# Pair 0's operand sums and remainders in halves on VectorE and GpSimd, layer one's on VectorE

## The chip, the cores and the metric

The kernel runs on one core of a Trainium2 chip. The metric is the device time of one execution in microseconds (us); lower is better. The engines are TensorE (PE in the profile, its weight loads PEld), VectorE (DVE), ScalarE (ACT), GpSimd (POOL) and SyncE (SP), whose queue starts nearly all DMAs.

## The reference

Sparse attention, then two dense layers, all in float32:

```python
scores = scale * q @ k.T                     # 4 batches, 8 heads, 576 positions, 64 wide
thresh = max(scores) - tau                   # per row
scores = where(scores >= thresh, scores, -1e9)
attn = softmax(scores); x = attn @ v         # x becomes 2304 tokens x 512
x = ((x @ w_a) * (x @ w_b)) @ w_out          # layer one, 1536 hidden
h = x @ w_in                                 # layer two, 1024 hidden
solu = h * softmax(h)
out = (layer_norm(solu) * g_ln) @ w_out2
```

## The kernel before

Attention handles two heads of one batch at a time in nine tiles of scores, and works them off two tiles to a step: 144 tiles, steps m = 0 to 77, scores up to step 71. In a step the engines work as follows. PE makes two tiles of scores (L586), the products with v of an older step (PV, L668) and the transposes of the step before (L637). DVE reduces each score tile out of PSUM into SBUF and finds its row minimum of the negated scores (`soft_max`, L591). ACT takes the exponential (L603). GpSimd makes a threshold of one column from the minimum (`soft_thr`, L608). DVE then masks (`soft_mask`, L617): scores and exponentials, both in SBUF, are compared with the threshold, multiplied and summed. The order of emission within a step is the string `PROG = 'ABtuVFTUYXfab'`: A and B are scores, reduction and exponential of the two tiles, t and u the thresholds, f the place for side work, a and b the masks.

Every float32 product of layer one is made from numbers split into a rounded high part and a remainder, so that three matmuls stand for one. Layer one uses Strassen's scheme with seven products (`product`, L510). The tokens are handled in three pairs of blocks of 384 columns. A pair's operands are made by normalising x (`norm_ops`, L386, L391, L395), four sums (`sum_ops`, L420), seven high parts on ACT and seven remainders (`operand_ops`, L444 and L448), and the seven are also stored for reuse (`store_op`). A sum or remainder covers 2 x 384 = 768 columns. The weights are converted from raw words, differenced (L276) and split (`split_ops`, L233 and L236).

Pair 0's operands are made during attention. Loads of x and of the softmax sums are issued at step 46. The pieces stand in the string `SLOTS` (n normalisation, s sum, h high part, l remainder, o store, z and x the loads of pair 1), and from step 52 on each step takes from its front: up to one piece of DVE, two of GpSimd, and one of ACT. A piece marked "DP" (VectorE or GpSimd) goes to GpSimd here. Pair 1's normalisation is appended at step 72 and runs two to a step. The conversion of the weights of layer one's first blocks is emitted at the end of steps 6 to 77 (`conv_emit`), its DVE part in `fill`.

In layer one (`moe1`) the order of the products, of the copies out of PSUM and of the gating multiplications is written out by unit n = 0 to 35; everything else is a task with a due time, which a planner (`bg`, `step`, `force`) places on the engines it may use, by a model of their costs and clocks. Pairs 1 and 2 get their operands there, and so do the weights after the first. A "DP" piece goes to whichever of the two engines the planner finds free. Each engine runs its instructions in the order of emission.

Of the kernel before, what the change touches and what calls it, by code (L numbers as in the profile page):

```python
# [17 lines left out]
P = 128  # L18
# [3 lines left out]
def kernel(  # L22
# [186 lines left out]
    def stage_ops(got, dst, low_of):  # L209
# [18 lines left out]
            return [("A", 512, expo), ("D", 300, low), ("D", 512, sign), ("D", 512, join)]  # L228
        return [("A", 512, lambda: nc.scalar.activation(out=dst(), in_=got["raw"], func=AF.Copy))]

    def split_ops(dst, src, n):
        def hi():
            nc.scalar.activation(out=dst(0), in_=src(), func=AF.Copy)  # L233

        def lo(e):
            (nc.vector if e == "D" else nc.gpsimd).tensor_tensor(out=dst(1), in0=src(), in1=dst(0).bitcast(F32), op=ALU.subtract)  # L236

        return ("A", n, hi), ("DP", n, lo)

    own = {}  # L240
    last = {}
# [8 lines left out]
    def ab_tasks(f, due, at, stage_at=0, bufs=("a", "t"), deps=()):  # L250
        ba, bt = bufs
        got = {}
        deps = list(deps) + [last[b] for b in bufs if b in last]
        la, lb = (load_w(w1[f, :, i], due - 16 + i, stage_at) for i in range(2))

        def view(b):
            if b not in got:
                got[b] = buffer(b).rearrange("p (o h c) -> p o h c", o=2, h=2)
            return got[b]

        def flat(b, i):
            return view(b)[:, i].rearrange("p h c -> p (h c)")

        def wt(o, u):
            if f not in wst:
                wst[f] = pools["w" if f % 4 < FW else "w4"].tile([P, 7, 2, QK * P], F32R, tag="w", name=f"w1_{f}")
            return wst[f][:, o, u, :]

        ta = task(due - 12, stage_ops(la["got"], lambda: flat(ba, 0), lambda: flat(bt, 0)), [la["load"]] + deps)
        tb = task(due - 10, stage_ops(lb["got"], lambda: flat(ba, 1), lambda: flat(bt, 0)), [lb["load"], ta])  # L270
        la["used"], lb["used"] = ta, tb
        a = lambda: view(ba)
        t = lambda: view(bt).rearrange("p o h c -> p (o h) c")

        def diff(n, out, x, y):
            return ("DP", n, lambda e: (nc.vector if e == "D" else nc.gpsimd).tensor_tensor(out=out(), in0=x(), in1=y(), op=ALU.subtract))  # L276

        td = task(due - 7, [
            diff(512, lambda: t()[:, 0:2], lambda: a()[:, 1], lambda: a()[:, :, 0, :]),
            diff(256, lambda: t()[:, 2], lambda: a()[:, 1, 1], lambda: t()[:, 0]),  # L280
            diff(256, lambda: t()[:, 3], lambda: a()[:, 0, 1], lambda: t()[:, 2]),
        ], [tb])
        parts = [
            split_ops(lambda u: wt(slice(0, 2), u), lambda: a()[:, 0], 512),
            split_ops(lambda u: wt(slice(3, 5), u), lambda: t()[:, 0:2], 512),
            split_ops(lambda u: wt(2, u), lambda: a()[:, 1, 1], 256),
            split_ops(lambda u: wt(slice(5, 7), u), lambda: t()[:, 2:4], 512),
        ]
        ready_w[f] = [task(due, [hi, lo], [td], at) for hi, lo in parts]
        end = task(due, [("S", 0, lambda: None)], ready_w[f], at)  # L290
        for b in bufs:
            last[b] = end
        return end
# [111 lines left out]
    def quad(p, i, k):  # L405
        return xs[p][:, k * QK:(k + 1) * QK, i * H:(i + 1) * H]

    def sum_ops(s, p):
        def one(k, e):
            if k == 0:  # L410
                scs[s] = own["sc"].rearrange("p (s k c) -> p s k c", s=4, k=QK)
            a11, a12, a21, a22 = (quad(p, i, h) for i in range(2) for h in range(2))
            z = scs[s]
            out, a, b, op = (
                (0, a21, a22, ALU.add),
                (1, z[:, 0], a11, ALU.subtract),
                (3, a12, z[:, 1], ALU.subtract),
                (2, a11, a21, ALU.subtract),
            )[k]
            (nc.vector if e == "D" else nc.gpsimd).tensor_tensor(out=z[:, out], in0=a, in1=b, op=op)  # L420

        return [("DP", QK * H, lambda e, k=k: one(k, e)) for k in range(4)]

    ORDER = [(s, j) for s in range(SETS[-1] + 1) for j in range(7) if s <= NPR or s % 2 or j > 1]
    GATE = (-1, -1, 0, 1, 2, 4, 6)
# [9 lines left out]
            own["x2"] = raw_p.tile([P, 2, QK, 2, H], F32R, tag="xr0", name="xt2")  # L435
        return own["x2"][:, j]

    def operand_ops(s, j, p):
        def src():
            return scs[s][:, (0, 0, 0, 1, 3, 2)[j]] if j in (1, 3, 4, 5) else quad(p, j // 6, min(j // 2, 1))  # L440

        def hi():
            xts[s, j] = new_xt(s, j)
            nc.scalar.activation(out=xts[s, j][:, :, 0, :], in_=src(), func=AF.Copy)  # L444

        def lo(e):
            x = xts[s, j]
            (nc.vector if e == "D" else nc.gpsimd).tensor_tensor(out=x[:, :, 1, :], in0=src(), in1=x[:, :, 0, :].bitcast(F32), op=ALU.subtract)  # L448

        return [("A", QK * H, hi), ("DP", QK * H, lo)]  # L450

    def store_op(s, j, p):
        nc.sync.dma_start(out=opd[p][j], in_=xts[s, j].bitcast(F32))
# [74 lines left out]

    def attention():
        es, es_r = ExitStack(), ExitStack()  # L530
        slots = []
        conv_ops = conv_first()
        ps_a = es.enter_context(tc.tile_pool(name="ps_a", bufs=3, space=PSUM))
        px = es.enter_context(tc.tile_pool(name="px", bufs=2))
# [76 lines left out]
        def soft_mask(i, s, th):  # L611
            ns, pe = st[i, s]
            if s == 0:
                st[i, "z"] = sm.tile([P, NS], F32, name="z", bufs=2)
            z = st[i, "z"]
            pv = pe.rearrange("p (g s) -> p g s", g=2)
            nc.vector.scalar_tensor_tensor(out=pv, in0=ns, scalar=th, in1=pv, op0=ALU.is_le, op1=ALU.mult, accum_out=z[:, s:s + 1])  # L617
            st[i, s] = pe

        def recip(i):  # L620
# [117 lines left out]
                    conv_emit("D")  # L738

        conv_at = range(6, tot // 2 + 6)  # L740
        PROG = 'ABtuVFTUYXfab'
        SLOTS = "n0 n1 n2 n3 s0 h0 l0 h1 o0 l1 h2 o1 l2 s1 o2 s2 h3 l3 h4 o3 s3 l4 h5 o4 l5 h6 z0 o5 l6 x0 o6"
        for m in range(tot // 2 + 6):
            if m == 46:
                load_z(0)
                load_x(0)
                ops = {"n": norm_ops(0), "s": sum_ops(0, 0), "z": [("S", 0, lambda: load_z(1))], "x": [("S", 0, lambda: load_x(1))]}
                ops["h"], ops["l"] = zip(*(operand_ops(0, j, 0) for j in range(NX)))
                ops["o"] = [("S", 0, lambda j=j: store_op(0, j, 0)) for j in range(NX)]
                slots = [ops[w[0]][int(w[1])] for w in SLOTS.split()]  # L750
                late = norm_ops(1)
            if m == tot // 2:
                es_s.close()
# [33 lines left out]
            for ch in PROG:  # L787
                if ch in "AB":
                    score("AB".index(ch))
                elif ch == "V":  # L790
                    for mm in mms:
                        mm()
                elif ch == "F":
                    for j in range(NP):
                        if m - j * NS // 2 == 8:
                            finish(j)
                elif ch in "TU":
                    turn("TU".index(ch))
                elif ch == "Y":
                    for c in old:  # L800
                        tpose_tail(*c)
                elif ch in "tu":
                    thr("tu".index(ch))
                elif ch in "ab":
                    mask("ab".index(ch))
                elif ch == "X":
                    if m == tot // 2:
                        for j in range(3):
                            product(0, 0, j)
                elif ch == "f":  # L810
                    fill(len(lo_old))
                    quota = {"D": 1, "P": 2, "A": 1, "S": 9}
                    if m == tot // 2:
                        slots += late
                        alloc_x(2)
                        quota["D"] = 2
                    while m >= 52 and slots and quota[slots[0][0][-1]]:
                        engs, _, fn = slots.pop(0)
                        eng = engs[-1]
                        quota[eng] -= 1  # L820
                        if len(engs) > 1:
                            fn = lambda fn=fn: fn("P")
                        if eng in "AS":
                            evac_q.append(fn)
                        else:
                            fn()
                        if eng == "A":
                            break
                    fill(1)
            for fn in dma_q + later:  # L830
                fn()
            dma_q.clear()
# [14 lines left out]
                    step(t)  # L847
            if m in conv_at:
                conv_emit("AP", 3)
        conv_emit("ADP", len(conv_ops))  # L850
        for t in ready_w[FW]:
            force(t)
        for engs, _, fn in slots:
            fn("P") if len(engs) > 1 else fn()
        for t in tasks:
            t["end"] = 0.0
        for e in clock:
# [24 lines left out]
    def moe1():  # L882
# [2 lines left out]
        gp = es.enter_context(tc.tile_pool(name="gp", bufs=1))  # L885
        yp = es.enter_context(tc.tile_pool(name="yp", bufs=4))
        groups = []
        ysteps = []
        stores = []

# [346 lines left out]
```

## Time and profile before

| | |
|---|---|
| median of 3 runs | 945.89 us (945.88 to 945.93) |
| the profiled execution | 946.57 us, of which the span in the profile is 944.8 us |
| PE busy | 908.5 us, 96% of the span |
| DVE busy | 654.3 us, 69% |
| ACT busy | 471.9 us, 50% |
| POOL busy | 283.0 us, 30% |

Times in the profile count from the start of the span. A busy PE is not a PE at its peak, since matmuls are pipelined and their ends are modelled. In the timelines a line gives start, duration, engine, line of the kernel, operation, output<-inputs, shape, count, and in brackets how long the engine had been idle and what ended that. Durations of neighbours on DVE overlap a little.

### The profile page before, as it was taken

Reading aid. Unit: us, or ns where it says so; the run is one execution under the profiler, and the core shown is the slowest. Engines: PE = TensorE matmul, PEld = TensorE weight load, DVE = VectorE, ACT = ScalarE, POOL = GpSimd, SP = SyncE. Lnnn points to the kernel's source line nnn. Section 1 sums busy time; section 2 is a strip of 40 time slices with the busy share of each in tenths; the row PEclk is TensorE's granted clock in tenths of the full one; section 3 lists DMA queues with packets and bytes.
Section 4 is the critical chain, followed back from the end, with each engine's and each line's share of the span. In section 5 each row is a group of like instructions: output and inputs, shape, how many; then the busy total and the mean of one; then the engine's idle time right before and its main releaser. Section 6 shows DMA issues by size and latency. Waiting matters only on the chain.

```text
span 944.8 us, 16336 instructions
## 1 busy us (share of the span) xinstructions
PE 908.5 (96%) x5896; PEld 752.5 (80%) x5896; DVE 654.3 (69%) x1359; ACT 471.9 (50%) x886; POOL 283.0 (30%) x347
## 2 busy tenths in 40 slices
PE   7999999998898788999999999999999899999998
PEld 3555565654468788999999999999998788888886
DVE  6999988899876775675668666876676544444443
ACT  5887877876775363543233323433342433333332
POOL 1255321136426352321023102110033433333330
PEclk9999999999999898999999999999999899999999
DMA  6435333845714847459765788568875011111100
GB/s 174 147 102 164 120 109 95 200 120 200 237 63 145 248 158 280 151 172 353 288 231 169 263 299 291 185 203 323 290 245 165 23 45 46 45 44 45 45 23 34
DMA packets 78481, 154.54 MB, mean 164 GB/s; under 512 B 11840, under 2 KB 51392, under 8 KB 78400
## 3 DMA queue, kind: packets, MB, share of 16 engines
q1 hardware_dynamic: 77600, 152.81, 48.9%
q8 instruction: 47, 0.77, 0.3%
q10 hardware_dynamic: 800, 0.68, 0.3%
q14 instruction: 34, 0.28, 0.1%
HBM read 108.55 MB, written 44.92 MB: 162 GB/s over the span
## 4 chain that ended last, share of the span: by engine, by line
PE 87%; DVE 7%; DMA 2%; issue 1%; ACT 1%; ACTq 0%; SPq 0%; POOL 0%; DVEq 0%; POOLq 0%
PE acc L510 26%; PE py L933 15%; PE po L1144 10%; PE ps L1088 9%; PE po L668 8%; PE ps L586 8%; PE tp L637 7%; DVE pe L617 3%; PE pl L1125 2%; PE py L510 1%; DVE ns L591 1%; DMA yd<-y 1%; PE tq L653 1%; DMA q<-in_qkv_dram 1%; DVE xt L448 1%
## 5 line engine op out<-in xcount | busy, mean ns | idle before, releaser
L510 PE MATMUL acc<-xt,w 128*128 128x384 f32 x1446 | 275.4, 340 | 6.5 <-DVE xt L448 5.6
L510 PEld LDWEIGHTS acc<-xt,w 128*128 128x128 f32 x1446 | 258.8, 191 | 7.7 <-DVE xt L448 6.2
L617 DVE SCALAR_TENSOR_TENSOR pe<-ns,th,pe 128x576 f32<-128x576 f32 x128 | 117.7, 951 | 7.7 <-ACT pe L603 6.6
L603 ACT ACTIVATE pe<-ns,nm 128x576 f32<-128x576 f32 x128 | 94.0, 775 | 52.1 <-DVE ns L591 51.7
L591 DVE TENSOR_SCALAR_CACHE_REDUCE ns<-ps 128x576 f32<-128x576 f32 x144 | 103.2, 752 | 10.7 <-PE ps L586 10.2
L586 PE MATMUL ps<-k,q 64*64 64x288 f32 x1152 | 93.2, 430 | 5.2 <-DMA k<-in_qkv_dram 3.5
L608 POOL TENSOR_SCALAR th<-nm,toff 128x1 f32<-128x1 f32 x144 | 45.0, 314 | 173.5 <-DVE ns L591 168.0
L933 PE MATMUL py<-ga,wo 128*128 128x384 f32 x432 | 86.2, 340 | 4.6 <-DVE wo L236 4.6
L1144 PE MATMUL po<-w,lt 128*128 128x512 f32 x378 | 90.0, 392 | 0.0
L933 PE MATMUL py<-gb,wo 128*128 128x384 f32 x432 | 84.0, 334 | 0.0
L1144 PEld LDWEIGHTS po<-w,lt 128*128 128x128 f32 x378 | 70.8, 188 | 15.6
L933 PEld LDWEIGHTS py<-ga,wo 128*128 128x128 f32 x432 | 77.7, 192 | 4.9 <-DVE wo L236 4.9
L637 PEld LDWEIGHTS tp<-ident,pe 128*128 128x128 f32 x512 | 56.4, 142 | 31.5 <-issue 15.8
L668 PE MATMUL po<-pt,vr 128*64 128x322 f32 (+1 forms) x512 | 78.8, 423 | 1.2 <-ACT xp L676 0.8
L637 PE MATMUL tp<-ident,pe 128*128 128x128 f32 x512 | 73.5, 281 | 6.2 <-DVE pe L617 5.2
L951 ACT ACTIVATE c<-acc 128x384 f32<-128x384 f32 x69 | 33.8, 492 | 91.1 <-PE acc L510 69.0
L630 ACT ACTIVATE pt<-tp 128x512 f32<-128x512 f32 (+1 forms) x160 | 78.0, 546 | 1.6 <-PE tp L637 1.0
L933 PEld LDWEIGHTS py<-gb,wo 128*128 128x128 f32 x432 | 75.7, 188 | 0.0
L1088 PE MATMUL ps<-w,ys 128*128 128x512 f32 x270 | 72.8, 401 | 0.0
L668 PEld LDWEIGHTS po<-pt,vr 128*64 128x64 f32 x512 | 33.2, 137 | 42.3 <-issue 18.1
L586 PEld LDWEIGHTS ps<-k,q 64*64 64x64 f32 x1152 | 36.5, 135 | 35.7 <-DVE ns L591 13.1
L1096 DVE TENSOR_REDUCE nm<-ps 128x1 f32<-128x1024 f32 x18 | 22.0, 1223 | 59.3 <-PE ps L1088 59.1
(138 smaller groups left out, 1307.7 us busy)
## 6 DMA issues: line engine op xcount, KB each, us to landing
xt<-opd SPq DMA_DIRECT2D x42, 768.0 KB
wraw<-in_w_dram SPq DMA_DIRECT2D x36, 512.0 KB
opd<-xt SPq DMA_DIRECT2D x21, 768.0 KB
ypd<-y SPq DMA_DIRECT2D x72, 192.0 KB
y<-ypd SPq DMA_DIRECT2D x72, 192.0 KB
q<-in_qkv_dram SPq DMA_DIRECT2D x15, 576.0 KB
k<-in_qkv_dram SPq DMA_DIRECT2D x30, 176.0 KB
xd<-xp SPq DMA_DIRECT2D x16, 289.0 KB
```

Of the source, the lines that this page charges most:

```text
L510: nc.tensor.matmul(ps, lhsT=w[:, WOP[j], wi, c * P:(c + 1) * P], rhs=x[:, c, xi, :], start=(k == 0 and j < 3), stop=(k == 3 * QK - 1 and j ...
L586: nc.tensor.matmul(ps[t * D:(t + 1) * D, g, 0:HS], lhsT=q[r, u, c], rhs=k[r, u, o:o + HS], start=True, stop=True, skip_group_check=True)
L591: nc.vector.tensor_scalar(out=ns, in0=st[i, s][:, :, 0:HS], scalar1=-SCALE, scalar2=None, op0=ALU.mult, op1=ALU.min, accum_out=nm)
L603: nc.scalar.activation(out=pe.rearrange("p (g s) -> p g s", g=2), in_=ns, func=AF.Exp, bias=nm, scale=-1.0)
L608: nc.gpsimd.tensor_scalar(out=th, in0=nm, scalar1=1.0, scalar2=toff, op0=ALU.mult, op1=ALU.add)
L617: nc.vector.scalar_tensor_tensor(out=pv, in0=ns, scalar=th, in1=pv, op0=ALU.is_le, op1=ALU.mult, accum_out=z[:, s:s + 1])
L630: evac_q.append(lambda: nc.scalar.activation(out=out, in_=in_, func=AF.Copy))
L637: nc.tensor.transpose(tp[:, kc, :], pe[:, o:o + P], ident)
L668: nc.tensor.matmul(po[h * D:(h + 1) * D], lhsT=lhsT, rhs=rhs, start=(kc == 0), stop=(kc == NQ), skip_group_check=True)
L933: nc.tensor.matmul(g["py"], lhsT=wos[g["q"] * F1 + r][:, wi, oc * P:(oc + 1) * P], rhs=g["g"][r][:, gi, :], start=(r == c == 0), stop=last ...
L1088: nc.tensor.matmul(ph[:, g, :], lhsT=y[:, a, kc, :], rhs=w2(2 * kc + g, b), start=(k == 0), stop=(k == 3 * KC - 1))
L1144: nc.tensor.matmul(po, lhsT=lt[:, a, j, :], rhs=w2(2 * KC + j, b), start=(k == 0), stop=(k == 3 * NJ - 1))
```

## The change

The 11 sums and remainders of pair 0 are split in two halves of 384 columns. The DVE half is emitted at place f of the step. The GpSimd half is kept back (`bulk`) and emitted behind the step's masks; it gets a dependence on the step's last mask (`gate`), as does all GpSimd work emitted through `two` at the end of a step of attention, the conversion's differences and remainders among it. The pieces follow a fixed table of steps (`STEPS`) from step 51 on, with one sum or remainder in a step, instead of quotas; the table ends at step 66. Pair 1's normalisation starts at step 69, one piece to a step, and two from step 72. Outside pair 0, sums and operand remainders are for DVE alone, and from layer one on the remainders of weights too; the differences of weights stay "DP". Pair 0's normalisation takes the order n0, n2, n1, n3.

```diff
+    gate = []
+
+    def two(e, part, out, in0, in1, op):
+        out, in0, in1 = ((a[part] if part else a) for a in (out, in0, in1))
+        got = (nc.vector if e == "D" else nc.gpsimd).tensor_tensor(out=out, in0=in0, in1=in1, op=op)
+        if e == "P" and gate:
+            tc.add_manual_dep(got.ins, gate[-1].ins.name, mybir.DependencyInfo(mybir.DependencyClass.Sync, mybir.DependencyReason.DATA), reason="gate")
...
-        return ("A", n, hi), ("DP", n, lo)
+        return ("A", n, hi), (("D", n, lambda: lo("D")) if late_w[0] else ("DP", n, lo))
...
-            (nc.vector if e == "D" else nc.gpsimd).tensor_tensor(out=z[:, out], in0=a, in1=b, op=op)
-
-        return [("DP", QK * H, lambda e, k=k: one(k, e)) for k in range(4)]
+            two(e, (slice(None), half), z[:, out], a, b, op)
+
+        if halves:
+            return [[("P", H, lambda k=k: one(k, "P", 0)), ("D", H, lambda k=k: one(k, "D", 1))] for k in range(4)]
+        return [("D", QK * H, lambda k=k: one(k, "D")) for k in range(4)]
...
-        return [("A", QK * H, hi), ("DP", QK * H, lo)]
+        if halves:
+            return [[("A", QK * H, hi)], [("P", H, lambda: lo("P", 0)), ("D", H, lambda: lo("D", 1))]]
+        return [("A", QK * H, hi), ("D", QK * H, lambda: lo("D"))]
...
-            nc.vector.scalar_tensor_tensor(out=pv, in0=ns, scalar=th, in1=pv, op0=ALU.is_le, op1=ALU.mult, accum_out=z[:, s:s + 1])
+            last_mask[0] = nc.vector.scalar_tensor_tensor(out=pv, in0=ns, scalar=th, in1=pv, op0=ALU.is_le, op1=ALU.mult, accum_out=z[:, s:s + 1])
...
-        SLOTS = "n0 n1 n2 n3 s0 h0 l0 h1 o0 l1 h2 o1 l2 s1 o2 s2 h3 l3 h4 o3 s3 l4 h5 o4 l5 h6 z0 o5 l6 x0 o6"
+        STEPS = (
+            "n0", "n2", "n1", "n3",
+            "s0 h0", "l0 h1", "l1 h2 o0", "l2 o1", "s1 o2", "s2 h3",
+            "l3 h4", "s3 o3", "l4 h5", "l5 h6 o4", "l6 z0 o5", "x0 o6",
+        )
...
-                    quota = {"D": 1, "P": 2, "A": 1, "S": 9}
                     if m == tot // 2:
-                        slots += late
                         alloc_x(2)
-                        quota["D"] = 2
-                    while m >= 52 and slots and quota[slots[0][0][-1]]:
...
+                    if m >= 51 and slots:
+                        for eng, _, fn in slots.pop(0):
+                            if eng == "D":
+                                fn()
+                            else:
+                                (bulk if eng == "P" else evac_q).append(fn)
+                    elif m >= 69 or m >= tot // 2:
+                        for _ in range(1 if m < tot // 2 else 2):
+                            if late:
+                                late.pop(0)[2]()
                     fill(1)
+            if cur:
+                gate.append(last_mask[0])
+            for fn in bulk:
+                fn()
+            bulk.clear()
...
             if m in conv_at:
                 conv_emit("AP", 3)
+            gate.clear()
...
+        late_w[0] = 1
```

## Rows read from the trace of the kernel before

**Rows 1.** Windows: us, then busy PE, PEld, DVE, ACT, POOL, PEclk, DMA share, GB/s.
```profile
204.90:248.85 43.95, 35.78 (x319) 18.30 (x318) 42.11 (x79) 29.93 (x56) 30.43 (x29) 1.00 0.49 166
...
276.10:318.35 42.25, 34.13 (x194) 30.16 (x193) 31.49 (x46) 20.51 (x42) 26.01 (x14) 0.95 0.46 163
318.35:376.10 57.75, 52.15 (x263) 51.52 (x264) 37.38 (x54) 26.57 (x50) 19.74 (x11) 0.89 0.65 218
376.10:706.98 330.88, 330.88 (x1897) 330.88 (x1897) 225.74 (x400) 126.39 (x248) 63.47 (x51) 1.00 0.71 246
```

**Rows 2.** Windows of nine steps of attention, from PV group to PV group.
```profile
69.76:103.02 33.26, 33.19 (x316) 18.83 (x318) 32.02 (x83) 27.37 (x55) 15.22 (x25) 1.00 0.40 126
...
145.65:177.51 31.86, 31.86 (x316) 18.75 (x318) 27.22 (x77) 25.20 (x49) 4.81 (x18) 1.00 0.43 114
```

**Rows 3.** The chain that ended last, steps 59 and 60: start, us, what.
```profile
226.49 2.38 DVE pe L617 x3
...
231.20 2.40 DVE pe L617 x3
```

**Rows 4.** Timeline of DVE, steps 52 to 59.
```profile
194.55 0.81 DVE L617 SCALAR_TENSOR_TENSOR pe<-ns,th,pe 128x576 f32<-128x576 f32 x1
...
206.53 0.81 DVE L617 SCALAR_TENSOR_TENSOR pe<-ns,th,pe 128x576 f32<-128x576 f32 x1
...
211.22 0.82 DVE L617 SCALAR_TENSOR_TENSOR pe<-ns,th,pe 128x576 f32<-128x576 f32 x1 [0.24 <-ACT pe L603]
...
223.72 0.75 DVE L591 TENSOR_SCALAR_CACHE_REDUCE ns<-ps 128x576 f32<-128x576 f32 x1
```

**Rows 5.** Timeline of POOL, steps 53 to 59, and layer one.
```profile
197.64 0.69 POOL L608 TENSOR_SCALAR th<-nm,toff 128x1 f32<-128x1 f32 x1 [0.41 <-DVE ns L591]
...
223.13 2.34 POOL L420 TENSOR_TENSOR sc<-sc,xr 128x768 f32<-128x768 f32 x1
225.44 0.51 POOL L608 TENSOR_SCALAR th<-nm,toff 128x1 f32<-128x1 f32 x2
...
350.02 1.86 POOL L420 TENSOR_TENSOR sc<-x 128x768 f32<-128x768 f32 x1
```

**Rows 6.** Timeline of PE: scores of step 52, PV of step 72, waits.
```profile
190.94 1.20 PE L586 MATMUL ps<-k,q 64*64 64x288 f32 x16
...
276.07 1.08 PE L668 MATMUL po<-pt,vr 128*64 128x256 f32 x8
...
318.35 1.01 PE L933 MATMUL py<-ga,wo 128*128 128x384 f32 x2 [4.58 <-DVE wo L236]
...
354.83 5.84 PE L510 MATMUL acc<-xt,w 128*128 128x384 f32 x23 [3.46 <-DVE xt L448]
```

**Rows 7.** Timeline of DVE at the start of layer one.
```profile
286.84 0.56 DVE L1001 TENSOR_TENSOR c<-py,c 128x384 f32<-128x384 f32 x1 [5.20 <-ACT c L951]
...
290.83 2.03 DVE L218 TENSOR_SCALAR st_a<-wraw 128x512 uint32<-128x512 uint32 x1
...
297.87 0.55 DVE L1033 TENSOR_TENSOR gb<-c,gb 128x384 fp32r<-128x384 f32 x1
...
306.07 2.35 DVE L225 SCALAR_TENSOR_TENSOR st_t<-st_t 128x512 uint32<-128x512 uint32 x1
...
316.55 1.74 DVE L236 TENSOR_TENSOR wo<-st_a,wo 128x512 fp32r<-128x512 f32 x1
...
352.21 2.56 DVE L448 TENSOR_TENSOR xt<-x,xt 128x768 fp32r<-128x768 f32 x1
...
355.57 0.94 DVE L448 TENSOR_TENSOR xt<-x,xt 128x768 fp32r<-128x768 f32 x1
...
362.08 2.57 DVE L448 TENSOR_TENSOR xt<-sc,xt 128x768 fp32r<-128x768 f32 x1
...
372.48 0.42 DVE L218 TENSOR_SCALAR sc<-wraw 128x512 uint32<-128x512 uint32 x1
```

**Rows 8.** Timeline of SP: pair 1's load of x.
```profile
247.59 1.42 SPq L373 DMA_DIRECT2D xr<-xd  x2
```

More of the change, by code (lines that the diff above doesn't have):

```diff
@@ L235, in lo @@
         def lo(e):
-            (nc.vector if e == "D" else nc.gpsimd).tensor_tensor(out=dst(1), in0=src(), in1=dst(0).bitcast(F32), op=ALU.subtract)
-        return ("A", n, hi), ("DP", n, lo)
+            two(e, (), dst(1), src(), dst(0).bitcast(F32), ALU.subtract)
+        return ("A", n, hi), (("D", n, lambda: lo("D")) if late_w[0] else ("DP", n, lo))
     own = {}
@@ L275, in diff @@
         def diff(n, out, x, y):
-            return ("DP", n, lambda e: (nc.vector if e == "D" else nc.gpsimd).tensor_tensor(out=out(), in0=x(), in1=y(), op=ALU.subtract))
+            return ("DP", n, lambda e: two(e, (), out(), x(), y(), ALU.subtract))
         td = task(due - 7, [
@@ L406, in quad, with sum_ops, one @@
         return xs[p][:, k * QK:(k + 1) * QK, i * H:(i + 1) * H]
-    def sum_ops(s, p):
-        def one(k, e):
+    def sum_ops(s, p, halves=False):
+        def one(k, e, half=slice(None)):
             if k == 0:
@@ L436, in new_xt, with operand_ops @@
         return own["x2"][:, j]
-    def operand_ops(s, j, p):
+    def operand_ops(s, j, p, halves=False):
         def src():
@@ L444, in hi, with lo @@
             nc.scalar.activation(out=xts[s, j][:, :, 0, :], in_=src(), func=AF.Copy)
-        def lo(e):
+        def lo(e, half=slice(None)):
             x = xts[s, j]
-            (nc.vector if e == "D" else nc.gpsimd).tensor_tensor(out=x[:, :, 1, :], in0=src(), in1=x[:, :, 0, :].bitcast(F32), op=ALU.subtract)
-        return [("A", QK * H, hi), ("DP", QK * H, lo)]
+            two(e, (slice(None), half), x[:, :, 1, :], src(), x[:, :, 0, :].bitcast(F32), ALU.subtract)
+        if halves:
+            return [[("A", QK * H, hi)], [("P", H, lambda: lo("P", 0)), ("D", H, lambda: lo("D", 1))]]
+        return [("A", QK * H, hi), ("D", QK * H, lambda: lo("D"))]
     def store_op(s, j, p):
@@ L530, in attention @@
         es, es_r = ExitStack(), ExitStack()
-        slots = []
+        slots, late, bulk = [], [], []
         conv_ops = conv_first()
@@ L740, in attention @@
         conv_at = range(6, tot // 2 + 6)
+        last_mask = [None]
         PROG = 'ABtuVFTUYXfab'
-        SLOTS = "n0 n1 n2 n3 s0 h0 l0 h1 o0 l1 h2 o1 l2 s1 o2 s2 h3 l3 h4 o3 s3 l4 h5 o4 l5 h6 z0 o5 l6 x0 o6"
+        STEPS = (
[3 more added lines that the diff above has]
+        )
         for m in range(tot // 2 + 6):
@@ L746, in attention @@
                 load_x(0)
[L747 to L750, printed above, removed]
+                ops = {"n": [[x] for x in norm_ops(0)], "s": sum_ops(0, 0, True), "z": [[("S", 0, lambda: load_z(1))]], "x": [[("S", 0, lambda: load_x(1))]]}
+                ops["h"], ops["l"] = zip(*(operand_ops(0, j, 0, True) for j in range(NX)))
+                ops["o"] = [[("S", 0, lambda j=j: store_op(0, j, 0))] for j in range(NX)]
+                slots = [[x for w in st.split() for x in ops[w[0]][int(w[1])]] for st in STEPS]
                 late = norm_ops(1)
@@ L811, in attention @@
                     fill(len(lo_old))
-                    quota = {"D": 1, "P": 2, "A": 1, "S": 9}
                     if m == tot // 2:
-                        slots += late
                         alloc_x(2)
-                        quota["D"] = 2
-                    while m >= 52 and slots and quota[slots[0][0][-1]]:
[L818 to L828, printed above, removed]
-                    fill(1)
+                    if m >= 51 and slots:
[8 more added lines that the diff above has]
+                                late.pop(0)[2]()
+                    fill(1)
+            if cur:
[3 more added lines that the diff above has]
+            bulk.clear()
             for fn in dma_q + later:
@@ L852, in attention @@
             force(t)
-        for engs, _, fn in slots:
-            fn("P") if len(engs) > 1 else fn()
+        for st_ in slots:
+            for _, _, fn in st_:
+                fn()
+        for _, _, fn in late:
+            fn()
         for t in tasks:
```

1 line of the change is left out of this document (added).

## The prediction

> **What bounds the kernel now.** I read the busy time by stretch first [rows 1]: it shows that no one engine sets the end throughout. From 376.10 to 706.98 us, layer one's steady part, PE is busy without a break and everything else hides behind it. From 204.90 to 248.85 PE is busy only 35.78 of 43.95 us while DVE is busy 42.11 and POOL 30.43. From 276.10 to 376.10, where layer one starts, PE is idle 8.12 + 5.60 = 13.7 us, and its clock was granted at 0.95 and 0.89 of full. These two places are where the change works; the last layer is not touched by it.
>
> Next I cut attention into stretches of nine steps, from the start of one PV group to the start of the same group nine steps on [rows 2]. Undisturbed, nine steps take 31.86 us and PE is busy all of it: 3.54 us a step. While layer one's first weights are converted beside them they take 33.26, 3.70 a step, and PE still is busy all but 0.07. Then the chain of waits: from 204 us on it runs through DVE, and from one step's second mask to the next, 226.49 to 231.20, are 4.71 us [rows 3].
>
> The timelines of DVE and POOL say why. A mask without company takes 0.81 us (206.53) [rows 4]; the second mask of a step with a GpSimd sum or remainder takes 2.38 [rows 3]. GpSimd's instruction starts right after the step's second threshold, so it lands on the masks, and the second mask does not end before it does. The score reduction L591 is another matter: the one at 223.72 takes its usual 0.75 us [rows 4] in the middle of a GpSimd sum that starts at 223.13 and takes 2.34 [rows 5]. So GpSimd work under the masks costs the step 2.38 - 0.81 = 1.57 us, and the same work under the reductions costs DVE nothing.
>
> **Pair 0's steps.** The change cuts each of the 11 pieces (four sums, seven remainders), one in each of steps 55 to 65, into a GpSimd half behind the second mask and a DVE half ahead of the first. Removed: the stretch; 4.71 - 1.57 = 3.14 us are left. Added on DVE: an instruction of 384 columns with both inputs in SBUF, 0.55 us (297.87) [rows 7], some 0.47 net, since neighbours overlap by about 0.08. Part of it fits where DVE now waits 0.24 for the exponential (211.22) [rows 4]. Step on DVE: 3.14 + 0.47 - 0.24 = 3.37 us, less than PE's 3.54. The GpSimd half has no row; half of 2.34 (223.13) and half of 1.86 (350.02) [rows 5] bound it at 1.17 and 0.93 us. It runs under two reductions, 2 x 0.68 = 1.36 us net, and is nearest to the first row, taken beside reductions too. Behind it on POOL queue the two thresholds of the next step, and the masks wait for those; with an estimated 0.2 us for the hand-over from DVE the half ends 1.4 us after the mask, and a threshold of 0.27 (225.44, two in 0.51) [rows 5] brings 1.67, before the first mask could start at 1.36 + 0.47 = 1.83. So that wait is hidden, by 0.16 us.
>
> With DVE off the chain, what is late next is PE itself, with ACT close behind, since the seven high parts stay there. I price the 11 steps as in the stretch that also carried side work on ACT and DVE: 3.70. The steps with a normalisation (three of pair 0 from step 52 on, three of pair 1 moved up to steps 69 to 71) take 3.99 by the masks 194.55 and 206.53, three steps apart [rows 4], but DVE has slack to lend, so they lie between 3.54 and 3.99: 3.8. Three plain steps at 3.54. From the scores of step 52 (190.94) to the PV of step 72 (276.07) [rows 6] are 85.1 us now. Afterwards 11 x 3.70 + 6 x 3.8 + 3 x 3.54 = 74.1. Gain 11.0 us. Bounds: every step at 3.54 gives 70.8, a gain of 14.3; halves at 3.95 (masks late by a threshold) and normalisations at 3.99 give 78.0, a gain of 7.1.
>
> Two covers can go. Pair 1's load is issued at 247.59 [rows 8], and its first normalisation came only after step 72; now it is wanted three steps behind the issue, some 11 us, with two stores in the same queue. A wait there stalls DVE with the masks behind it; between 0 and 3 us, I take 0.5, because the shortened steps bring load and use to nearly the same clock times as before. And the gate also holds the conversion's GpSimd work of the earlier steps behind the last mask. That frees masks which are stretched now, and makes a chain of three GpSimd instructions start later, with thresholds behind it: by estimate -1 to +1 us, hidden by PE's queue (PE is idle 0.07 us in nine such steps [rows 2]) and taken as 0. Attention: -10.5, bounds -15.3 and -3.1.
>
> By the Trainium skill (SBUF — State Buffer, Who interferes with whom) GpSimd and a DVE instruction with two SBUF inputs exclude each other for the whole instruction, whichever starts first. It speaks against the DVE half, which would then shut out the threshold queued behind the GpSimd half: first mask at 1.9 + 0.27 = 2.2 instead of 1.83, a step of 3.75. The row of a threshold that took 0.69 instead of 0.27 beside a normalisation (197.64) [rows 5] agrees. By the rule the 11 steps cost 0.6 us more, by the sum above nothing.
>
> **Start of layer one.** Sums and remainders of pairs 1 and 2 go to DVE alone. A remainder of 768 columns takes 0.94 us there without company (355.57) and up to 2.57 (362.08) with a GpSimd one running [rows 7]; the GpSimd one itself takes 1.86 or more [rows 5]. PE's waits here end on such instructions. (a) Pair 2: 352.21 takes 2.56 and 362.08 takes 2.57, and PE waits 3.46 us for the first (354.83) [rows 6]. Without company each shrinks by 1.6: -3.2. (b) Pair 1: five DVE instructions from 306.07 to 316.55 [rows 7] are stretched by 6.1 us together, and PE waits 4.58 (318.35) [rows 6]; but five remainders come over, 5 x 0.87 net = 4.4: -1.7. (c) At 290.83 a weight conversion takes 2.03 instead of the 0.42 of 372.48 [rows 7]: -1.6; the sums that replace GpSimd's fit into the 5.20 us in which DVE idles before 286.84 [rows 7], since pair 1's normalisation is then past. Sum -6.5. The lower clock cost 0.05 x 42.25 + 0.11 x 57.75 = 8.5 us on top of 13.7 of waits, 0.62 for each; a shortened wait need not give it back, so I count a third: -1.3. Together -7.8. Bounds: nothing, if what comes over fills DVE as much as the stretch did; and all 13.7 + 8.5 = 22.2.
>
> **Steady layer one.** GpSimd's remainders of the weights, part of its 51 instructions in 376.10 to 706.98 [rows 1], also go to DVE. DVE idles 331 - 226 = 105 us there and PE hides the work: 0. If that cover fails, see the slower rival.
>
> **Sum.** The profiled execution took 946.57 us (span 944.8 and 1.8 around it), 0.7 above the median of 945.89. 946.57 - 10.5 - 7.8 = 928.3, so 928; the 0.7 is far inside the range. The forecast's own range has the larger unknown, the start of layer one, half way to its bounds (-3.9 and -15.0): 921 to 932.
>
> **Rivals.** *Only attention gains* (18%): DVE stays full at the start of layer one, and new waits replace the old ones. For it: stretch and moved work nearly cancel in (b). Against: the waits end on single stretched instructions. 946.6 - 10.5 = 936, with half of attention's spread 932 to 940. *The waits at the start vanish altogether* (14%): 946.6 - 10.5 - 22.2 = 914, up to 921 if a third of it stays. *The halves do nothing* (5%): the GpSimd half is late each time, thresholds and masks follow it and a step stays near 4.7; for it speaks the cover of only 0.16 us. What is left is between nothing and part (a): 943 to 947, half of it within 0.2%. *Slower* (4%): a remainder in front of the PSUM evacuations of layer one holds PE up in every unit. At 0.55 us apiece for 51 of them it costs 28 us: 946.6 - 18.3 + 28 = 956. It decides from 18.3 / 51 = 0.36 us apiece on. Against it: PE's unbroken 331 us beside a DVE that idles for a third.
>
> **Chances.** Forecast 59%, the rest as above. About 0.2% is what a measurement can tell from no change here. Faster by more: 59 + 18 + 14 + half of 5 = 93%; the same 3%, slower 4%. The range reaches into both faster rivals, to 917 and 938.
>
> **What would show it.** Second masks of steps 55 to 65 at 0.81, GpSimd halves of 0.9 to 1.2 us under L591, a step of 3.5 to 3.8, PV of step 72 near 266: then the attention part is right. First masks that wait for the threshold, a first normalisation of pair 1 that waits for its load, or a step above 4: wrong. In layer one no operand remainder or sum on POOL, 0.94 us each on DVE, and shorter waits of PE; if PE waits for them as long as now, the first rival holds. A PE with breaks in its steady part would be the slower one.

## The result, and the profile after

The changed kernel takes 918.86 us, median of four executions (915.14 to 919.32), beside 945.88 for the kernel before in the same series (943.75 to 945.93). The ratio is 0.9711, with a 95% interval of 0.9682 to 0.9740. The forecast was 928, its own range 921 to 932, the whole range 917 to 938.

The profiled execution took 918.58 us; its span is 916.7 us, 28.1 shorter. PE is busy 894.6 us of it (98%), DVE 645.0 (70%), POOL 181.1 (20%). To see where the 28.1 us went I set the same groups of matmuls side by side in the two timelines of PE. The line numbers have moved: the scores are L600 now, the reduction L605, the threshold L622, the mask L631, and all sums and remainders go through `two`, L235.

| stretch | before | after | difference | forecast |
|---|---|---|---|---|
| start to scores of step 52 | 190.94 | 190.44 | -0.5 | 0 |
| to the PV of step 72 | 85.13 | 74.71 | -10.4 | -10.5 |
| to a matmul group of unit 7 (376.79, now 350.18) | 100.72 | 85.03 | -15.7 | -7.8 |
| to the last units (706.82, now 680.21) | 330.03 | 330.03 | 0.0 | 0 |
| to the end of the span | 237.98 | 236.49 | -1.5 | 0 |

The 0.5 us of the first row say nothing: among the kernels below whose program is the change's up to there, the scores of step 52 start at 190.16 to 191.01.

The timeline of PE after, with the same groups as [rows 6] and the waits that are left:

```profile
190.44 1.20 PE L600 MATMUL ps<-k,q 64*64 64x288 f32 x16
...
259.35 0.66 PE L651 MATMUL tp<-ident,pe 128*128 128x128 f32 x4 [1.17 <-DVE pe L631]
...
265.15 1.08 PE L682 MATMUL po<-pt,vr 128*64 128x256 f32 x8
...
282.62 1.33 PE L524 MATMUL py<-xt,w 128*128 128x384 f32 x6 [1.92 <-DVE c L1044]
...
298.20 3.24 PE L524 MATMUL acc<-xt,w 128*128 128x384 f32 x17 [1.47 <-DVE xt L235]
...
304.13 1.15 PE L524 MATMUL acc<-xt,w 128*128 128x384 f32 x5 [0.78 <-DVE xt L235]
...
333.74 4.30 PE L524 MATMUL acc<-xt,w 128*128 128x384 f32 x23 [0.77 <-DVE xt L235]
```

The wait of 4.58 us in [rows 6], for the remainder of a weight (`wo`), is gone; at that place PE now waits 1.47 and 0.78 us for remainders of pair 1 (`xt`). The wait of 3.46 us for pair 2's first remainder has become 0.77. The wait of 1.92 us ends on an addition out of PSUM and was 2.68 before. The remainder behind the wait of 0.77, in the timeline of DVE after, takes 0.95 us, where the one of 352.21 in [rows 7] took 2.56:

```profile
332.74 0.95 DVE L235 TENSOR_TENSOR xt<-x,xt 128x768 fp32r<-128x768 f32 x1
```
The windows after (columns as in [rows 1]; the third holds nine of pair 0's steps):

```profile
265.15:350.00 84.85, 79.23 (x460) 75.03 (x460) 67.23 (x113) 48.44 (x95) 13.88 (x11) 1.00 0.65 221
350.00:678.00 328.00, 328.00 (x1882) 328.00 (x1881) 229.57 (x431) 125.12 (x246) 13.70 (x14) 1.00 0.71 249
...
209.85:241.71 31.86, 31.86 (x319) 18.75 (x315) 30.87 (x88) 29.29 (x56) 15.65 (x27) 1.00 0.56 193
```

The first line is the start of layer one: PE is idle 84.85 - 79.23 = 5.6 us where it was idle 13.7, and its clock is granted at 1.00 where it was 0.95 and 0.89 [rows 1]. The second is the steady part: PE without a break, DVE at 70%, and on POOL 14 instructions are left of 51. In the third PE has no break either, and nine steps take the 31.86 us of the undisturbed nine in [rows 2].

The timelines of DVE and POOL after, two of the steps with halves:

```profile
208.78 0.55 DVE L235 TENSOR_TENSOR xt<-xr,xt 128x384 fp32r<-128x384 f32 x1
...
209.25 0.82 DVE L631 SCALAR_TENSOR_TENSOR pe<-ns,th,pe 128x576 f32<-128x576 f32 x1
...
209.99 0.81 DVE L631 SCALAR_TENSOR_TENSOR pe<-ns,th,pe 128x576 f32<-128x576 f32 x1
...
211.41 0.75 DVE L605 TENSOR_SCALAR_CACHE_REDUCE ns<-ps 128x576 f32<-128x576 f32 x1
...
212.09 0.55 DVE L235 TENSOR_TENSOR xt<-sc,xt 128x384 fp32r<-128x384 f32 x1
```

```profile
210.89 1.01 POOL L235 TENSOR_TENSOR xt<-xr,xt 128x384 fp32r<-128x384 f32 x1 [1.44 <-DVE pe L631]
211.88 0.27 POOL L622 TENSOR_SCALAR th<-nm,toff 128x1 f32<-128x1 f32 x1
212.34 0.43 POOL L622 TENSOR_SCALAR th<-nm,toff 128x1 f32<-128x1 f32 x1 [0.19 <-DVE ns L605]
```

Both masks take their plain 0.81, where the second took 2.38 [rows 3]; the reduction keeps its 0.75 beside the GpSimd half, which takes 1.01. From one DVE half to the next are 212.09 - 208.78 = 3.31 us.

### The profile page after: what moved, and what is told of

Same layout as the page of the kernel before. It is cut to its first block, busy times and chain, and to the rows that moved or that the text cites. A ratio compares the mean times of both kernels' runs of the same rounds, so it can differ in the third digit from the quotient of the medians.

```text
span 916.7 us, 16293 instructions
## 1 busy us (share of the span) xinstructions
PE 894.6 (98%) x5896; PEld 745.0 (81%) x5896; DVE 645.0 (70%) x1425; ACT 471.3 (51%) x886; POOL 181.1 (20%) x292
## 4 chain that ended last, share of the span: by engine, by line
PE 79%; DVE 10%; DMA 3%; issue 3%; ACT 3%; POOL 1%; SPq 1%; ACTq 0%; DVEq 0%; POOLq 0%
PE acc L524 26%; PE py L957 15%; PE po L1168 10%; PE ps L1112 10%; PE po L682 5%; PE ps L600 5%; PE tp L651 5%; DVE pe L631 3%; DVE ns L605 3%; PE pl L1149 2%; DMA y<-ypd 1%; DMA opd<-xt 1%; POOL st_t L235 1%; DVE xt L235 1%; PE py L524 1%
## 5 line engine op out<-in xcount | busy, mean ns | idle before, releaser
L524 PE MATMUL acc<-xt,w 128*128 128x384 f32 x1446 | 270.6, 336 | 3.0 <-DVE xt L235 3.0
L524 PEld LDWEIGHTS acc<-xt,w 128*128 128x128 f32 x1446 | 254.4, 188 | 4.0 <-DVE xt L235 4.0
L605 DVE TENSOR_SCALAR_CACHE_REDUCE ns<-ps 128x576 f32<-128x576 f32 x144 | 103.1, 751 | 9.2 <-PE ps L600 8.9
L631 DVE SCALAR_TENSOR_TENSOR pe<-ns,th,pe 128x576 f32<-128x576 f32 x128 | 100.1, 813 | 6.2 <-ACT pe L617 3.8
L600 PE MATMUL ps<-k,q 64*64 64x288 f32 x1152 | 90.2, 424 | 5.3 <-DMA k<-in_qkv_dram 3.5
L957 PE MATMUL py<-ga,wo 128*128 128x384 f32 x432 | 84.0, 334 | 0.0
L622 POOL TENSOR_SCALAR th<-nm,toff 128x1 f32<-128x1 f32 x144 | 47.7, 333 | 158.8 <-DVE ns L605 153.3
L651 PEld LDWEIGHTS tp<-ident,pe 128*128 128x128 f32 x512 | 56.5, 143 | 26.1 <-issue 10.0
L957 PEld LDWEIGHTS py<-ga,wo 128*128 128x128 f32 x432 | 75.7, 188 | 0.0
L600 PEld LDWEIGHTS ps<-k,q 64*64 64x64 f32 x1152 | 37.3, 134 | 32.1 <-issue 6.5
```

Of the source, the lines that this page charges most:

```text
L524: nc.tensor.matmul(ps, lhsT=w[:, WOP[j], wi, c * P:(c + 1) * P], rhs=x[:, c, xi, :], start=(k == 0 and j < 3), stop=(k == 3 * QK - 1 and j ...
L600: nc.tensor.matmul(ps[t * D:(t + 1) * D, g, 0:HS], lhsT=q[r, u, c], rhs=k[r, u, o:o + HS], start=True, stop=True, skip_group_check=True)
L605: nc.vector.tensor_scalar(out=ns, in0=st[i, s][:, :, 0:HS], scalar1=-SCALE, scalar2=None, op0=ALU.mult, op1=ALU.min, accum_out=nm)
L622: nc.gpsimd.tensor_scalar(out=th, in0=nm, scalar1=1.0, scalar2=toff, op0=ALU.mult, op1=ALU.add)
L631: last_mask[0] = nc.vector.scalar_tensor_tensor(out=pv, in0=ns, scalar=th, in1=pv, op0=ALU.is_le, op1=ALU.mult, accum_out=z[:, s:s + 1])
L651: nc.tensor.transpose(tp[:, kc, :], pe[:, o:o + P], ident)
```

## The experiments

Each kernel was timed beside the kernel before on the same chip, which had medians of 945.15, 944.26 and 945.05 us in the three series. The change itself was timed in a series of its own (945.88). Differences of medians under some 3 us lie within the intervals and settle nothing by themselves.

**The change without its part in layer one.** Only pair 0's steps stay changed:

```diff
-        return [("D", QK * H, lambda k=k: one(k, "D")) for k in range(4)]
+        return [("DP", QK * H, lambda e, k=k: one(k, e)) for k in range(4)]
-        return [("A", QK * H, hi), ("D", QK * H, lambda: lo("D"))]
+        return [("A", QK * H, hi), ("DP", QK * H, lo)]
-        late_w[0] = 1
+        late_w[0] = 0
```

> Pair 0's halves, the gate and the moved normalisation as in the change; sums and remainders of layer one go to VectorE or GpSimd as before. Theory A (the two parts are separate, and layer one gains because GpSimd no longer stretches VectorE's instructions there): the attention part alone, 85.1 - 74.7 = 10.4 us and the 0.5 ahead of it, so 934 to 936 us, with the lower clock of 0.9 at the start of layer one still there. Theory B (layer one gains because pair 1's normalisation is past when it starts, and its sums can go ahead): nearly the whole gain, 919 to 923 us.

Measured: 936.29 us (933.66 to 937.95), ratio 0.9910 (0.9878 to 0.9942). PE waits in layer one as it did before, as its timeline shows:

```profile
308.93 1.01 PE L957 MATMUL py<-ga,wo 128*128 128x384 f32 x2 [4.59 <-DVE wo L235]
...
344.73 6.39 PE L524 MATMUL acc<-xt,w 128*128 128x384 f32 x23 [4.06 <-DVE xt L235]
```

Attention alone is worth 8.9 us, and the start of layer one gives nothing without its own edit.

**The kernel before with only the part in layer one.** Sums and remainders of pairs 1 and 2 and the late remainders of weights go to VectorE; pair 0's steps stay as they were:

```diff
+        if not both:
+            return [("D", QK * H, lambda k=k: one(k, "D")) for k in range(4)]
         return [("DP", QK * H, lambda e, k=k: one(k, e)) for k in range(4)]
...
+        if not both:
+            return [("A", QK * H, hi), ("D", QK * H, lambda: lo("D"))]
         return [("A", QK * H, hi), ("DP", QK * H, lo)]
...
+        late_w[0] = 1
```

> The kernel before with sums and remainders of layer one (pairs 1 and 2 and the weights from the fourth block on) on VectorE alone; pair 0 whole on GpSimd in attention. Theory A: the 15.7 us that the start of layer one gained and the 1.5 at the end, so 928 to 931 us, with a full clock from the last step of attention on. Theory B: little without the earlier normalisation, 940 to 945 us.

Measured: 927.93 us (927.24 to 929.98), ratio 0.9827 (0.9800 to 0.9855), 17.2 us. The two parts add up: 8.9 + 17.2 = 26.1, and the whole change gives 945.88 - 918.86 = 27.0. Its timeline of PE has the same wait of 1.92 us as the change, but the six matmuls behind it take 2.21 us instead of 1.33. The full clock that I had expected there was not granted: it is 0.53 from 291.96 to 294.10.

```profile
291.96 2.21 PE L516 MATMUL py<-xt,w 128*128 128x384 f32 x6 [1.92 <-DVE c L1027]
```

**Which of the moved pieces counts in layer one.** First the weights' remainders alone go back to either engine (`late_w[0] = 0`), then the pairs' sums and remainders alone (the first four lines of the first diff).

> The change with the remainders of layer one's weights on VectorE or GpSimd, as before; sums and remainders of pairs 1 and 2 stay on VectorE. Theory A (the pairs carry the gain): within 1 us of the change. Rival (it takes GpSimd out of layer one altogether): GpSimd stretches VectorE at the start again, 2 to 6 us longer.

> The change with sums and remainders of pairs 1 and 2 on VectorE or GpSimd, as before; the weights' remainders stay on VectorE. Theory A: most of the 15.7 us of layer one's start are lost, 930 to 935, with waits of PE for remainders of 3 us and more and a lower clock. Rival (the weights matter as much): 5 to 8 us lost.

Measured: 920.59 us (920.36 to 923.30, ratio 0.9755, 0.9729 to 0.9782) with the weights back, 933.74 (931.27 to 935.00, ratio 0.9885, 0.9857 to 0.9913) with the pairs back. The pairs' operands carry the gain, and with them back PE waits 2.68, 4.58 and 3.46 us again. What the weights add is within the intervals. With the weights back PE's waits at the start of layer one are those of the change; the six matmuls behind the wait of 1.92 us take 2.15 us, and from the PV of step 72 to the wait of 1.47 us it loses 1.5 us against the change. The last section shows the same fall of the clock in a kernel that does not differ from the change at this place, so I cannot put it down to the weights.

**The halves without the gate.**

```diff
-            if cur:
-                gate.append(last_mask[0])
```

> The change without the gate: GpSimd work at the end of a step no longer waits for the last mask. If the gate keeps GpSimd off the masks (theory A): the half of 1.0 us lands under the masks again, a mask of 0.81 takes up to 1.5, steps 55 to 65 go from 3.32 to about 3.9 on VectorE against PE's 3.5, so 4 to 6 us longer than the change: 922 to 925. If the split alone does it (rival: half the length, half the stretch, which PE's slack takes): within 1 us of the change.

Measured: 923.19 us (922.03 to 924.73), ratio 0.9770 (0.9738 to 0.9801), within what I had expected of theory A; its interval just touches the change's. Timelines of POOL and DVE of this kernel:

```profile
206.31 1.51 POOL L235 TENSOR_TENSOR sc<-xr 128x384 f32<-128x384 f32 x1
```

```profile
206.13 0.82 DVE L631 SCALAR_TENSOR_TENSOR pe<-ns,th,pe 128x576 f32<-128x576 f32 x1
...
206.88 1.55 DVE L631 SCALAR_TENSOR_TENSOR pe<-ns,th,pe 128x576 f32<-128x576 f32 x1
```

Without the gate the half starts behind the second threshold, on the first mask. It takes 1.51 instead of 1.00 us, and the second mask 1.55 instead of 0.81: the half lasts longer by what is left of the first mask, the second mask by what is then left of the half. By the Trainium skill (SBUF — State Buffer, Who interferes with whom) one of the two holds the shared port for its whole instruction and the other waits; these rows agree. From one first mask to the next (206.13 to 210.19) are 4.06 us instead of 3.31, and the PV of step 72 comes 79.23 us behind the scores of step 52, where the change has 74.71.

**The gate with whole pieces on GpSimd.**

```diff
-            return [[("P", H, lambda k=k: one(k, "P", 0)), ("D", H, lambda k=k: one(k, "D", 1))] for k in range(4)]
+            return [[("P", QK * H, lambda k=k: one(k, "P"))] for k in range(4)]
...
-            return [[("A", QK * H, hi)], [("P", H, lambda: lo("P", 0)), ("D", H, lambda: lo("D", 1))]]
+            return [[("A", QK * H, hi)], [("P", QK * H, lambda: lo("P"))]]
```

> The change with pair 0's sums and remainders whole on GpSimd behind the last mask, none on VectorE. If the thresholds queued behind the GpSimd instruction set the step (theory A): it takes 1.9 to 2.3 us from 0.2 after the mask, the threshold ends 2.5 us after the mask instead of 1.5, the masks wait for it, a step of 4.1 to 4.3: 11 x 0.7 = 7 to 9 us longer than the change, 925 to 928. If the gate alone does it (rival: nothing on VectorE is lost while GpSimd runs under the reductions): the same as the change within 1 us.

Measured: 920.82 us (918.96 to 922.93), ratio 0.9749 (0.9720 to 0.9779): faster than theory A had it, and 2 us above the change, where the rival had the same within 1 us; the intervals overlap. POOL and DVE of this kernel:

```profile
207.76 1.83 POOL L235 TENSOR_TENSOR sc<-xr 128x768 f32<-128x768 f32 x1 [1.44 <-DVE pe L631]
209.56 0.51 POOL L622 TENSOR_SCALAR th<-nm,toff 128x1 f32<-128x1 f32 x2
```

```profile
209.87 0.82 DVE L631 SCALAR_TENSOR_TENSOR pe<-ns,th,pe 128x576 f32<-128x576 f32 x1 [0.84 <-ACT pe L617]
...
213.63 0.82 DVE L631 SCALAR_TENSOR_TENSOR pe<-ns,th,pe 128x576 f32<-128x576 f32 x1 [0.84 <-ACT pe L617]
```

The whole piece takes 1.83 us under the reductions, not the 2.34 of [rows 5]. The two thresholds come behind it, and the first mask starts when the first of them is done (the row names ACT as the releaser; the threshold ends later). The step is 213.63 - 209.87 = 3.76 us. The PV of step 72 comes 78.35 us behind the scores of step 52, beside 74.71: counted like this, pair 1's load is issued 3.4 us later, and DVE waits 3.94 us for it, see below.

**All of pair 0's pieces on VectorE.** The same two lines, with `("D", QK * H, ...)`.

> The change with pair 0's sums and remainders whole on VectorE ahead of the first mask, none on GpSimd. Theory A: 0.40 us more on VectorE in each of 11 steps, 3.71 instead of 3.31, against PE's 3.5; as with the whole pieces on GpSimd (step 3.75) most of it hides in PE's queue, 1 to 3 us longer than the change, 920 to 922. Rival: without GpSimd there is nothing to exclude, no stretched threshold, and it is as fast as the change or faster.

Measured: 919.21 us (916.49 to 920.82), ratio 0.9740 (0.9710 to 0.9769). A DVE piece of 768 columns takes 0.95 us, the step is 3.71 us (3.77 on average over ten), and the PV of step 72 comes at 265.42, 0.27 later than with the halves. So most of the gain in attention comes from taking GpSimd off the masks. What the split adds does not show here; the next two experiments show why.

**Pair 1's normalisation later,** from step 72 on, two pieces to a step, as in the kernel before:

```diff
-                    elif m >= 69 or m >= tot // 2:
+                    elif m >= tot // 2:
```

> The change with pair 1's normalisation at step 72 again, two pieces to a step, as before. If the wait of 3.23 us that VectorE has for pair 1's load at step 69 reaches the end (theory A): it goes, and nothing takes its place, since VectorE idles 6.55 us ahead of layer one's first addition: 2 to 3.5 us shorter than the change, 915.5 to 917. If PE's queue hides that wait (rival), or the sums of pair 1 come late for it: within 1 us of the change, or longer.

Measured: 915.51 us (913.74 to 917.32, five executions), ratio 0.9698 (0.9674 to 0.9722). The wait that it takes away is this one, in the timeline of DVE of the change:

```profile
257.28 0.23 DVE L393 TENSOR_SCALAR vs<-vs,neg 128x8 f32<-128x8 f32 x1 [3.23 <-DMA vs<-xd]
```

The PV of step 72 comes at 262.58 instead of 265.15, 2.6 us earlier. This kernel is the fastest of all that I ran and beats the kernel before by 3%; its interval and the change's overlap, so the profile, not the time, is what says that it also beats the change.

**Both of the last two edits.**

> The change with two edits: pair 0's sums and remainders whole on VectorE (no half on GpSimd), and pair 1's normalisation from step 72 on, two pieces to a step, as in the kernel before. Theory A (the wait for pair 1's load hides what the split is worth, and with the load out of the way the steps themselves set the time): eleven steps at 3.71 instead of 3.48 show as 11 x 0.23 = 2.5 us more than the change with normalisation at step 72 alone: 917 to 919, PV of step 72 near 265. Rival B (VectorE whole is as good as the halves): 914.5 to 916.5, PV of step 72 near 263.

Measured: 918.43 us (915.89 to 919.25, five executions), ratio 0.9718 (0.9698 to 0.9738). The scores of step 52 and the PV of step 72 in the timelines of PE, first of this kernel, then of the one with halves and the later normalisation:

```profile
191.01 1.20 PE L600 MATMUL ps<-k,q 64*64 64x288 f32 x16
...
265.58 1.08 PE L682 MATMUL po<-pt,vr 128*64 128x256 f32 x8
```

```profile
190.41 1.20 PE L600 MATMUL ps<-k,q 64*64 64x288 f32 x16
...
262.58 1.08 PE L682 MATMUL po<-pt,vr 128*64 128x256 f32 x8
```

That is 74.57 us beside 72.17, so theory A held in the time and in the profile: with the load out of the way the halves save 2.4 us. Whole pieces on VectorE make a step of 3.77 us (206.04 to 243.71, ten steps), longer than PE's 3.54 [rows 2]; 11 x 0.23 = 2.5. In the medians it is 2.9 us, and there the intervals overlap.

**What a wait of PE costs.** Extra DVE instructions (the maximum of a tile with itself) ahead of one addition out of PSUM in units 20 and 26, where PE has no break; six of them, then 14:

```diff
+            for _ in range(6 if n in (20, 26) else 0):
+                nc.vector.tensor_tensor(out=tmp[1], in0=tmp[1], in1=tmp[1], op=ALU.max)
             free[n + 1, 2, 1] = tz[1] = crit("D", H, max(e4, tz[1]), lambda: nc.vector.tensor_tensor(out=tmp[1], in0=z, in1=tmp[1], op=ALU.add))
```

> The change with six extra VectorE instructions of 384 columns (some 0.47 us each, 2.8 us together, results unchanged) ahead of one addition out of PSUM in units 20 and 26 of layer one, in the steady part where TensorE has no break. It measures what a wait of TensorE costs there. Theory A (a wait costs its own length and some 0.6 us a us through the clock): with a wait of 1 to 2.5 us at each place the granted clock falls below 1.00 behind it and the time is 922 to 927. Rival B (a short wait costs only its length): clock stays 1.00, 920 to 923. Rival C (the buffers in PSUM swallow 2.8 us): no wait, 918 to 919.5.

> The same with 14 extra instructions (6.6 us) in units 20 and 26. Theory A: waits of TensorE of 3.5 to 6 us at each place, granted clock below 1.00 behind each, 7 to 12 us of waits and 4 to 7 us of clock: 930 to 938. Rival B: the same waits with the clock at 1.00: 926 to 931. Rival C (buffers swallow most): 919 to 924.

One execution each: 920.21 and 930.18 us, spans 918.3 and 928.2. PE with six extra instructions (3.52 us of DVE, 0.59 apiece, more than the 0.47 that I had reckoned):

```profile
510.28 2.38 PE L524 MATMUL acc<-xt,w 128*128 128x384 f32 x12 [0.66 <-DVE c L1046]
...
580.10 2.37 PE L524 MATMUL acc<-xt,w 128*128 128x384 f32 x12 [0.38 <-DVE c L1046]
```

and with 14 (8.27 us of DVE), its timeline and its windows:

```profile
510.50 1.81 PE L524 MATMUL acc<-xt,w 128*128 128x384 f32 x6 [3.35 <-DVE c L1037]
513.61 4.21 PE L524 MATMUL acc<-xt,w 128*128 128x384 f32 x12 [1.30 <-DVE c L1046]
...
587.33 2.29 PE L524 MATMUL acc<-xt,w 128*128 128x384 f32 x6 [3.36 <-DVE c L1037]
590.13 3.66 PE L524 MATMUL acc<-xt,w 128*128 128x384 f32 x12 [0.51 <-DVE c L1046]
```

```profile
510.00:530.00 20.00, 18.20 (x88) 17.70 (x89) 12.17 (x23) 6.19 (x13) 2.21 (x2) 0.83 0.70 246
530.00:550.00 20.00, 20.00 (x117) 20.00 (x116) 12.92 (x25) 5.80 (x11) 2.24 (x2) 1.00 0.75 257
```

Against the change's timeline, group by group, the short waits shift PE by 0.94 and 0.68 us: their length and some 0.3 each, with the clock at 1.00 in every window of 20 us from 510 to 650. The long ones shift it, up to the first group that is back at its usual length, by 7.62 and 6.72 us for 4.65 and 3.87 us of waits; at the second place the clock is 0.90 and 0.92 in the windows from 570 to 610. Less 0.3 for each of the four waits, 14.34 - 8.52 - 1.2 = 4.6 us are the clock's, half a microsecond for one of wait. So for the six instructions rival B held, with shorter waits than I had expected, and for the 14 theory A did, at the lower end of its numbers. The shifts are the evidence, more than the total of one execution, since the clock falls at other places too (last section). The span grows by 11.5 us and not by 14.3: the transition to the last layer is 2.8 us shorter here, with a shorter wait and without the change's fall of the clock, below.

## Why the prediction was right, point by point

**Pair 0's steps** (forecast 3.70 a step, 11 of them). The mechanism is as forecast in every row: masks at 0.81, the half under the reductions, thresholds hidden. DVE's step is 3.31 us where nothing waits, against my sum of 3.37; the GpSimd half takes 1.01, nearer to my lower bound of 0.93 than to the 1.17 that I had reckoned with, because the piece of 2.34 that it came from began while a mask still ran (221.42 + 2.37); a whole piece under the reductions takes 1.83. The price was off: I took 3.70, and nine steps of PE take 31.86 us without a break (window 209.85 to 241.71), 3.54 each, which is the floor of [rows 2] and my lower bound. The 11 steps were 11 x 0.16 = 1.8 us cheaper than forecast.

**The load of pair 1** (forecast 0.5 us, bounds 0 to 3). It cost 3.23 on DVE, in the row shown with that experiment, and 1.17 + 0.17 + 0.42 + 0.58 = 2.3 us of waits on PE behind it. The timeline of SP after shows the issues:

```profile
243.46 1.32 SPq L383 DMA_DIRECT2D xr<-xd  x2
244.82 3.20 SPq L386 DMA_DIRECT2D vs<-xd  x1
```

DVE comes for the load at 257.28 - 3.23 = 254.05, 10.6 us behind the first issue, as I had worked out (some 11), and gets it after 13.8. The distance was right; I had no row for how long the load takes, and took it for shorter. So the two errors, 1.8 us less for the steps and 1.8 more for the load, cancel: that -10.4 agrees with -10.5 is luck. From issue to use the load takes 13.1 to 14.0 us in all seven kernels whose waits for it I compared, and its issue comes right behind the end of pair 0's last remainder. With whole pieces on VectorE that is at 243.96, DVE comes later because its steps are longer, and it waits 1.22 us. With whole pieces on GpSimd the last remainder ends at 247.17, the issue is at 247.20, and DVE waits 3.94. The load's arrival sets the time there, and it hides differences between versions of the steps until the normalisation is moved: halves and whole pieces on VectorE differ by 0.4 us with it (74.71 and 75.14) and by 2.4 without.

**The rule against the DVE half.** The threshold behind the GpSimd half does lengthen, from 0.27 to 0.43 (212.34 above, beside the DVE half at 212.09 and ending 0.13 behind it). By the Trainium skill (SBUF — State Buffer, Who interferes with whom) the two exclude each other, and the row agrees; but the first mask does not wait for the threshold that it delays, which is the second, and the 0.6 us that I had worked out from the rule are not there.

**Start of layer one** (forecast -7.8, measured -15.7). This is the term that was mis-sized. Its waits shrank by 13.7 - 5.6 = 8.1 us where I had 6.5. By pieces, from matmul group to matmul group and with the clock's part in each: (a) pair 2 gave -8.2 us (I had -3.2 for the wait alone), (b) pair 1 -6.1 (I had -1.7), (c) -1.4, sum -15.7. Of (c) the wait itself gave nothing: the group behind it starts 17.31 us after the PV of step 72 before and 17.47 after; the 1.4 us are the faster matmuls behind it. The larger error is the clock: of its price for the waits that I took away I let a third come back, 1.3 us, and in this profile all of the stretch's loss came back, 15.7 - 8.1 = 7.6 us, with the clock at 1.00. The step "0.62 for each; a shortened wait need not give it back" is what failed: [rows 1] only show waits long enough to lower the clock, and a price per microsecond taken from those is not the price of short ones. The experiment with extra instructions shows both: behind waits of 0.38 and 0.66 us the clock stays at 1.00, behind 3.35 + 1.30 it is 0.83. The result of 918.86 therefore lies 2 us below the forecast's own range, where I had put the rival "the waits vanish altogether" (914 to 921), although 5.6 us of waits are left. The kernels with one part each, and those that put one group of pieces back, show that the gain belongs to pairs 1 and 2 going to VectorE. They do not separate how much of it is due to the unstretched instructions of VectorE and how much to the pieces coming in another order.

**Only attention gains.** This rival is the first experiment, 936.29 for a forecast of 936, but not the change. **The halves do nothing** is excluded by the steps, 3.54 us instead of 4.71, and **slower** by PE's 328.00 of 328.00 us busy in the steady part, with 14 POOL instructions left.

**The end.** 1.5 us come from the transition to the last layer, which the change does not touch: PE's wait there is 3.37 us and was 4.67. I had not forecast it, and no run here isolates it.

## What to carry to other kernels

When two engines slow each other, look which instructions of the one the other meets: the same GpSimd work cost 1.57 us a step under the masks and left the reductions out of PSUM at their 0.75 us. Ordering it behind the last mask took most of the loss away, and so did giving it to VectorE whole; with pair 1's load out of the way, halves instead of whole pieces on VectorE were worth another 2.4 us, since a step with the whole piece, 3.77 us, is longer than PE's 3.54. Price TensorE's waits by their length and, where they are long enough to lower the clock in the trace at hand, by the whole clock loss of the stretch: shortening such a wait may give all of it back at once. And when steps get shorter, ask for each load used behind them whether its issue moved by the same amount; here it cost 3.23 us, and a later use took that away.

## What the runs showed of the hardware

The length of a wait does not decide alone whether PE's clock falls. The same 1.92 us wait for an addition is followed by six matmuls in 1.33 us in the change and in 2.21 in the kernel with only the part in layer one. It is not the program that decides either: the kernel with six extra instructions is the change up to unit 20, far behind this place, and there the six take 2.05 us (1.31 in the one with 14). From the PV of step 72 to the next wait that execution takes 1.6 us longer than the change's. At the change's transition to the last layer the first window below has the clock at 0.91, and six matmuls of the scores of that layer take 2.91 us behind a wait of 3.37; in the kernel with 14 extra instructions they take 1.65 behind a wait of 2.76:

```profile
678.00:716.00 38.00, 34.63 (x166) 30.98 (x165) 27.85 (x51) 12.68 (x22) 7.70 (x7) 0.91 0.43 130
...
707.13 1.97 PE L1149 MATMUL pl<-ident,e 128*128 128x128 f32 x8 [3.37 <-DVE rz L1130]
708.75 2.91 PE L1112 MATMUL ps<-w,ys 128*128 128x512 f32 x6
```

```profile
720.63 1.09 PE L1151 MATMUL pl<-ident,e 128*128 128x128 f32 x8 [2.76 <-DVE rz L1132]
721.81 1.65 PE L1114 MATMUL ps<-w,ys 128*128 128x512 f32 x6
```

By the Trainium skill (TensorE: Matmul & The Clock Gate, Part 1: The HAM clock gate) the clock has two levels, 1.2 and 2.4 GHz; the granted clock from 708.75 to 711.60 us in the change is 0.50, the lower one, and six matmuls that take 1.52 us at full clock in the same layer take 2.91. What else decides is left open.
